# One attention-and-MLP kernel with a new order of its steps: scores of units 3 to 5 in split f16 products, one subtraction moved to VectorE, six sets of fillers fewer

## The chip, the cores and the metric

The kernel runs on one core of a Trainium2 chip. The metric is the device time of one execution in microseconds. TensorE (PE) multiplies matrices, VectorE (DVE) and ScalarE (ACT) work elementwise, GpSimd (POOL) reduces across partitions, and SyncE (SP) issues the DMAs. Each engine takes its instructions strictly in the order in which the program lists them.

## The reference

Attention over 4 batches of 8 heads, 768 positions and 64 dimensions. Each query sees the keys less than 16 positions away and 24 summary keys (maxima of blocks of 32). A two-layer MLP with exact gelu follows.

```python
k_sum = k.reshape(B, H, nb, block, D).max(axis=3)
v_sum = v.reshape(B, H, nb, block, D).mean(axis=3)
scores_l = scale * q @ k.T                    # kept where |i - j| < 16
scores_s = scale * q @ k_sum.T + np.log(block)
scores_all = concat(scores_l_masked, scores_s)
a = np.exp(scores_all - max(scores_all))
a = a / (sum(a) + 1e-9)
attn = a @ concat(v, v_sum)
h = x @ w_in                                  # x: (3072, 512), w_in: (512, 2048)
out = (gelu(h)) @ w_out                       # w_out: (2048, 512)
```

## The kernel before

The attention is cut into 24 units (a batch, four heads, 256 queries); four steps of units 0 to 5 make batch 0. Most products are **split**: an f32 operand becomes a high f16 part and a low one (the rest), and three f16 products (high by high, high by low, low by high) stand for one of f32. The low parts are all made on DVE, and the high ones on ACT: `x_hi` and `x_lo` for the attention's result, `wi_hi`, `wi_lo`, `wo_hi`, `wo_lo` for the weights, `g_hi`, `g_lo` for the gelu's output, and `q_lo`, `k_lo`, `p_lo`, `v_lo` for a unit's queries, keys, probabilities and values. The weights come as 64-bit floats and are turned into f32 by three integer steps each on DVE (`wi_bits`, `wo_bits`, steps 0 to 2); eight chunks of `w_in` and eight of `w_out`.

A unit's scores are either `f_scores` (line 688: 16 matmuls in f32 of a packed copy of the keys that `k_pack` makes on ACT, lines 669 and 675) or `scores` (line 756: 48 matmuls in f16, from `s_q_hi`, `q_lo`, `s_k_hi`, `k_lo`). Before, units 0 to 5 take the first, the others the second. `f_mask` puts the mask into PSUM ahead of them. `evac` copies the scores to SBUF, `maximum` takes the maximum over the partitions on POOL, and it is subtracted either by `m_shift` (line 736: a matmul of -1 with the maximum onto the scores in PSUM, whose result `m_exponent` reads) or by `shift` (line 790: a subtraction in SBUF on DVE, whose result `exponent` reads). Then come `f_sums` or `sums` (denominators), `f_values` or `values` (line 838), and the norm steps `norm_take`, `norm_cross`, `norm_rec`, `norm_spread`, `norm_mult`.

The MLP works on chunks of 256 rows (two units each): `phase1 c i` (lines 915 to 917) makes 256 columns of the hidden layer out of 24 matmuls of 256 columns, and `phase2 c i` (lines 1034 to 1036) makes a quarter of the sum of an output block out of 12 matmuls of 512 columns. `phase2` of quarter n reads the low parts `wo_lo 2n` and `wo_lo 2n+1`. Batches 2 and 3 and the last four chunks' output use a Strassen form (`sp`, line 986, and `so`, line 1199).

`fill` (line 337) is a set of three matmuls of ones into a tile that nobody reads; `setup` issues 16 more of them. They give nothing to the output.

What sets the order is one long text, `ORDER`: a list of some 1,680 steps, written out by hand, each a call of one of the functions named here. It fixes the order on every engine and on the DMA queue of SP. Tiles come from pools with a fixed count of buffers: scores have one tile in PSUM (`pss`) for all units but unit 1, queries one buffer in SBUF, values two.

Of the kernel before, what the change touches and what calls it, by code (L numbers as in the profile page):

```python
# [82 lines left out]
0, wi_bits 2 0, evac 2, load_ind, wi_bits 2 1, fetch_vt 0, sum_vt 0, norm_cross 0, norm_rec 0, maximum 2, fetch_vt 1,
norm_spread 0, m_shift 1, m_exponent 1, fetch_vt 2, load_v 0, sum_vt 1, sum_vt 2, wi_bits 2 2, wi_hi 2, wi_lo 4,
k_pack 3, m_shift 2, fill 12, fetch_w_in 3 3, wi_lo 5, wi_lo 2, wi_bits 3 0, load_v 1, mean_vt, wi_bits 3 1, f_sums 1,
s_load_vs 0, f_values 0, norm_mult 0, m_exponent 2, f_mask 3, load_q 3, f_scores 3, s_load_vs 1, norm_take 1, wi_bits
3 2, x_hi 0, x_lo 0, norm_cross 1, norm_rec 1, f_values 1, fill 13, evac 3, f_sums 2, norm_spread 1, norm_mult 1,
norm_take 2, fetch_w_in 1 1, wi_hi 3, x_hi 1, x_lo 1, fetch_w_out 1 5, norm_cross 2, wi_bits 1 0, norm_rec 2, phase1 0
4, wo_bits 1 0, wi_bits 1 1, load_q 6, maximum 3, m_shift 3, s_q_hi 6, wo_bits 1 1, wi_bits 1 2, phase1 0 2, fetch_k 2
1, prep_k 2 1, load_v 2, m_exponent 3, load_vs 2, wi_hi 1, fetch_w_in 7 3, norm_spread 2, q_lo 6, phase1 0 5, f_values  # L90
2, load_v 3, gelu 0 5, g_hi 0 5, wi_lo 1, load_vs 3, fetch_k 1 3, f_mask 4, wo_bits 1 2, gelu 0 2, load_k 4, g_hi 0 2,
norm_mult 2, k_pack 4, f_sums 3, gelu 0 4, norm_take 3, load_q 4, norm_cross 3, prep_k 1 3, wi_bits 7 0, phase1 0 1,
f_values 3, wi_lo 3, wi_bits 7 1, load_v 4, wo_hi 1, fetch_k 1 2, f_scores 4, x_hi 2, fetch_k 1 1, evac 4, norm_rec 3,
norm_spread 3, g_hi 0 4, prep_k 1 2, gelu 0 1, phase1 0 0, x_lo 2, norm_mult 3, x_hi 3, fetch_w_in 6 2, prep_k 1 1,
f_mask 5, load_vs 4, x_lo 3, g_lo 0 4, g_lo 0 5, fetch_w_out 0 4, fetch_w_out 3 5, wi_bits 6 0, phase1 0 3, maximum 4,
shift 4, wo_lo 1, load_k 5, wi_bits 6 1, g_hi 0 1, g_lo 0 1, gelu 0 0, g_hi 0 0, g_lo 0 0, phase1 1 4, fetch_v 1 2,
load_q 5, gelu 0 3, fetch_k 1 0, phase1 1 5, exponent 4, g_hi 0 3, wi_bits 7 2, f_values 4, gelu 1 5, wo_bits 0 0,
wi_bits 6 2, f_sums 4, g_hi 1 5, g_lo 1 5, wi_hi 7, k_pack 5, wo_bits 0 1, norm_take 4, wi_lo 7, phase1 1 1, load_v 5,
gelu 1 1, g_hi 1 1, g_lo 1 1, wi_hi 6, phase1 1 0, wi_lo 6, prep_v 1 2, load_vs 5, gelu 1 4, f_scores 5, phase1 1 7,
norm_cross 4, gelu 1 0, g_hi 1 0, evac 5, g_hi 1 4, g_lo 0 3, load_k 6, s_k_hi 6, norm_rec 4, wo_bits 0 2, maximum 5,  # L100
norm_spread 4, prep_k 1 0, g_lo 1 0, load_v 6, wo_bits 3 0, fetch_w_out 2 4, phase1 1 6, wo_hi 0, wo_bits 3 1, phase1
1 3, gelu 1 7, phase1 0 7, wo_lo 0, phase2 0 0, shift 5, gelu 1 3, g_hi 1 3, wo_bits 3 2, fetch_w_out 5 5, g_lo 1 3,
norm_mult 4, wo_bits 2 0, exponent 5, f_sums 5, prep_k_end 1 0, f_values 5, gelu 1 6, wo_bits 2 1, load_q 7, norm_take
5, wo_bits 2 2, k_lo 6, g_hi 1 7, g_lo 1 7, wo_hi 3, k_sums 1 0, wo_bits 5 0, wo_lo 3, phase1 0 6, g_lo 0 2, gelu 0 6,
g_hi 0 6, wo_bits 5 1, wo_hi 2, wo_lo 2, fetch_w_out 4 4, f_mask 6, wo_bits 4 0, wo_bits 4 1, norm_cross 5, norm_rec
5, phase1 1 2, gelu 0 7, wo_bits 4 2, wo_hi 4, wo_bits 5 2, wo_hi 5, prep_k_end 1 1, wo_lo 4, wo_lo 5, g_lo 1 4,
scores 6, fetch_v 1 0, phase2 0 1, phase2 0 3, norm_spread 5, load_k 7, s_k_hi 7, phase2 0 2, fetch_v 1 1, phase2 0 5,
g_hi 0 7, fetch_w_out 6 4, x_hi 4, fetch_w_out 7 5, x_lo 4, norm_mult 5, s_q_hi 7, prep_v 1 1, evac 6, maximum 6,
phase2 0 4, load_mask, x_hi 5, x_lo 5, load_v 7, f_mask 7, q_lo 7, gelu 1 2, k_sums 1 1, shift 6, exponent 6, phase1 2
3, g_lo 0 6, wo_bits 6 0, phase1 2 1, load_q 9, k_lo 7, gelu 2 3, wo_bits 7 0, wo_bits 6 1, scores 7, g_hi 1 2, g_lo 1  # L110
2, wo_bits 6 2, wo_bits 7 1, gelu 2 1, s_q_hi 9, wo_hi 6, g_lo 0 7, wo_lo 6, phase1 2 0, load_k 9, wo_bits 7 2, q_lo
9, phase1 2 4, s_k_hi 9, k_lo 9, fetch_v 1 3, gelu 2 0, g_hi 2 0, s_p_hi 6, wo_hi 7, wo_lo 7, phase1 2 6, load_q 11,
load_k 8, phase2 0 6, fetch_k 2 2, prep_v 1 0, g_hi 1 6, g_lo 2 0, s_q_hi 11, prep_v 1 3, q_lo 11, p_lo 6, phase2 0 7,
store 0 0, phase2 1 0, fetch_v 2 1, load_vs 6, load_q 8, evac 7, maximum 7, load_vs 7, s_k_hi 8, gelu 2 6, put 0 0,
g_lo 1 6, prep_v 2 1, sums 6, k_lo 8, fetch_k 2 0, gelu 2 4, g_hi 2 4, v_hi 6, scores 9, norm_take 6, phase2 1 2,
phase2 1 4, prep_k 2 2, shift 7, v_hi 7, v_lo 6, values 6, store 0 1, fetch_k 2 3, g_lo 2 4, g_hi 2 1, prep_k 2 0,
phase1 2 5, s_q_hi 8, q_lo 8, add_mask 9, v_lo 7, scores 8, exponent 7, s_p_hi 7, norm_cross 6, phase2 1 6, p_lo 7,
load_v 8, prep_k 2 3, put 0 1, g_hi 2 6, load_k 11, s_k_hi 11, add_mask 8, load_vs 8, v_hi 8, k_lo 11, norm_rec 6,
norm_spread 6, sums 7, norm_mult 6, x_hi 6, norm_take 7, v_lo 8, phase1 2 2, maximum 9, shift 9, load_q 10, maximum 8,
shift 8, store 1 0, prep_k_end 2 1, values 7, norm_cross 7, norm_rec 7, scores 11, exponent 8, x_lo 6, exponent 9,  # L120
s_q_hi 10, phase2 1 1, load_v 9, norm_spread 7, load_vs 9, gelu 2 5, load_k 10, load_v 11, phase2 1 3, g_lo 2 1,
add_mask 11, load_vs 11, norm_mult 7, g_hi 2 5, g_lo 2 6, s_p_hi 8, p_lo 8, g_hi 2 3, g_lo 2 3, x_hi 7, phase1 2 7,
s_k_hi 10, phase2 1 5, x_lo 7, v_hi 9, maximum 11, phase1 3 0, v_lo 9, gelu 2 7, wt_add 1 0, wt_add 1 1, wt_add 1 2,
wt_hi 1, k_lo 10, sums 8, shift 11, values 8, s_p_hi 9, q_lo 10, norm_take 8, norm_cross 8, load_v 10, gelu 3 0, g_hi
3 0, wt_lo 1, fetch_k 3 1, load_q 12, load_vs 10, norm_rec 8, phase1 3 4, phase2 1 7, wt_add 5 0, p_lo 9, phase1 3 1,
norm_spread 8, norm_mult 8, put 1 0, g_lo 3 0, gelu 2 2, exponent 11, scores 10, wt_add 5 1, fetch_k 3 2, g_hi 2 2,
g_lo 2 2, prep_k 3 1, x_hi 8, store 1 1, wt_add 5 2, g_hi 2 7, g_lo 2 7, gelu 3 4, prep_k 3 2, values 9, wt_hi 5, sums
9, norm_take 9, norm_cross 9, add_mask 10, s_p_hi 11, phase1 3 6, g_lo 2 5, gelu 3 6, load_k 12, phase2 2 1, wt_lo 5,
fetch_v 2 0, s_k_hi 12, norm_rec 9, phase1 3 2, norm_spread 9, put 1 1, gelu 3 1, phase1 3 5, x_lo 8, v_hi 11,
norm_mult 9, prep_k_end 2 0, maximum 10, s_q_hi 12, k_lo 12, shift 10, exponent 10, p_lo 11, q_lo 12, x_hi 9, load_k  # L130
13, s_k_hi 13, v_lo 11, gelu 3 2, k_lo 13, fetch_v 2 2, fetch_v 2 3, g_hi 3 1, phase2 2 3, phase2 2 5, g_hi 3 4,
prep_v 2 0, values 11, k_sums 2 0, k_sums 2 1, sums 11, wt_add 0 0, x_lo 9, phase2 2 7, wt_add 0 1, norm_take 11, sp 2
# [1211 lines left out]
```

## Time and profile before

| what | before |
|---|---|
| median of 3 runs | 575.72 us (575.28 to 575.73) |
| span of the profiled execution | 574.3 us |
| PE busy | 569.0 us (99%) |
| DVE busy | 458.4 us (80%) |
| ACT busy | 379.8 us (66%) |
| POOL busy | 88.7 us (15%) |
| granted TensorE clock, mean | 0.999 |

The span runs from the first to the last instruction of one profiled execution; the median is of timed runs, and lies 1.4 us above that span. A busy time of 99% says that PE almost always had a matmul in it, not that each of them was needed. The shares are means over the whole span: the first 140 us, in which the weights are prepared, are loaded otherwise than the rest.

### The profile page before, as it was taken

What the parts mean: (1) busy time and instruction counts of PE and PEld (TensorE: products, weight loads), DVE (VectorE), ACT (ScalarE), POOL (GpSimd) and SP (SyncE); (2) the same over time, 40 slices, a digit from 0 to 9 for tenths busy, and PEclk for the clock granted to TensorE, in tenths of its full rate; (3) what the DMA queues carried; (4) which work ended last, traced back from release to release, by engine and by line L of the source; (5) the groups of instructions that cost most, each with busy time, mean ns of one, the idle gap of its engine ahead of it and who ended that gap; (6) DMA issues with size and microseconds to landing.
All of it is one profiled execution on the core that took longest, in us unless ns stands there. A gap on an engine that the chain in (4) does not pass through costs nothing.

```text
span 574.3 us, 13533 instructions
## 1 busy us (share of the span) xinstructions
PE 569.0 (99%) x5826; PEld 389.8 (68%) x5826; DVE 458.4 (80%) x617; ACT 379.8 (66%) x642; POOL 88.7 (15%) x42
## 2 busy tenths in 40 slices
...
GB/s 322 395 238 250 342 175 196 274 116 198 159 115 99 141 79 71 115 121 76 103 93 66 72 105 56 60 98 78 23 63 1 21 19 18 1 20 1 2 1 91
DMA packets 28652, 64.27 MB, mean 112 GB/s; under 512 B 2736, under 2 KB 7600, under 8 KB 28592
## 3 DMA queue, kind: packets, MB, share of 16 engines
...
## 4 chain that ended last, share of the span: by engine, by line
PE 95%; DVE 4%; issue 1%; ACT 0%; POOL 0%; DVEq 0%; ACTq 0%; POOLq 0%
PE psy L986 15%; PE pso L1034 12%; PE pso L1035 12%; PE pso L1036 12%; PE psz L986 7%; PE psh L915 4%; PE psh L917 4%; PE psh L916 4%; PE psx L986 4%; PE pso_y L1199 4%; PE psv L838 3%; PE pss L756 3%; PE pss_x L1199 2%; PE pso_fill L337 2%; PE pss L688 1%; PE pso_fill_s L337 1%
## 5 line engine op out<-in xcount | busy, mean ns | idle before, releaser
L785 POOL PARTITION_ALL_REDUCE m<-s x23 | 77.4, 3370 | 303.5 <-DVE s L776 80.9
L1034 PE MATMUL pso<-w_out_h,gg 128*128 128x512 f16 x320 | 121.5, 380 | 0.0
L1035 PE MATMUL pso<-w_out_l,gg 128*128 128x512 f16 x320 | 121.3, 379 | 0.0
L1036 PE MATMUL pso<-w_out_h,gg 128*128 128x512 f16 x320 | 121.3, 379 | 0.0
L986 PEld LDWEIGHTS <-wt 128*128 128x128 f16 x768 | 74.4, 98 | 13.6 <-issue 1.1
L916 PE MATMUL psh<-xos,ww 128*128 128x256 f16 x256 | 69.8, 273 | 0.6 <-DVE xos L895 0.6
L915 PE MATMUL psh<-xos,ww 128*128 128x256 f16 x256 | 69.9, 273 | 0.0
L917 PE MATMUL psh<-xos,ww 128*128 128x256 f16 x256 | 69.8, 273 | 0.0
L986 PE MATMUL psy<-xos,wt 128*128 128x256 f16 x576 | 69.3, 273 | 0.0
L986 PEld LDWEIGHTS <-ww 128*128 128x128 f16 x576 | 55.4, 98 | 11.7 <-issue 0.4
L1036 PEld LDWEIGHTS <-gg 128*128 128x128 f16 x320 | 31.3, 98 | 37.8
L1034 PEld LDWEIGHTS <-gg 128*128 128x128 f16 x320 | 31.3, 98 | 33.2 <-issue 0.8
L1035 PEld LDWEIGHTS <-gg 128*128 128x128 f16 x320 | 31.3, 98 | 31.5
L1018 DVE SCALAR_TENSOR_TENSOR gg<-g,gg 128x512 f16<-128x512 f32 x48 | 34.7, 731 | 11.5 <-ACT gg L1014 11.4
L997 ACT ACTIVATE ww<-psy 128x512 f32<-128x512 f32 x48 | 28.1, 587 | 23.7 <-PE psy L986 23.4
L1041 ACT ACTIVATE ot<-pso 128x512 f32<-128x512 f32 x20 | 11.8, 592 | 29.3 <-PE pso L1036 29.3
L1014 ACT ACTIVATE gg<-g 128x512 f16<-128x512 f32 x48 | 29.4, 625 | 2.7 <-PE pso L1035 2.0
L1004 DVE TENSOR_TENSOR g<-psz,ww 128x512 f32<-128x512 f32 x24 | 16.4, 682 | 18.5 <-PE psz L986 15.8
L1011 ACT ACTIVATE g<-g 128x512 f32<-128x512 f32 x36 | 22.3, 623 | 10.8 <-DVE g L1004 10.7
L915 PEld LDWEIGHTS <-ww 128*128 128x128 f16 x256 | 25.0, 98 | 6.3 <-issue 2.2
L917 PEld LDWEIGHTS <-ww 128*128 128x128 f16 x256 | 25.0, 98 | 3.7 <-issue 0.7
L916 PEld LDWEIGHTS <-ww 128*128 128x128 f16 x256 | 25.0, 98 | 3.4
...
## 6 DMA issues: line engine op xcount, KB each, us to landing
...
```

Of the source, the lines that this page charges most:

```text
L785: nc.gpsimd.partition_all_reduce(out_ap=self.m32, in_ap=self.s32, channels=P, reduce_op=bass_isa.ReduceOp.max)
L915: nc.tensor.matmul(ph[:, e, :], wh, xh, start=(k == 0), stop=False)
L916: nc.tensor.matmul(ph[:, e, :], wh, xl, start=False, stop=False)
L917: nc.tensor.matmul(ph[:, e, :], wl, xh, start=False, stop=(k == NCC - 1))
L986: nc.tensor.matmul(ps[:, e, :], ws, xx, start=(first and e == 0 and k == 0 and m == 0), stop=(k == 1 and m == 2), skip_group_check=True,)
L997: nc.scalar.activation(snaps[b, q, n], split8(acc[b, q, "y"]), AF.Copy)
L1014: nc.scalar.activation(g_part(o // 2, q, 0, slice(o % 2, 4, 2)), g32t[b, q, o], AF.Copy, scale=SC_G)
L1018: nc.vector.scalar_tensor_tensor(out=g_part(o // 2, q, 1, fs), in0=g32t.pop((b, q, o)), scalar=SC_G, in1=g_part(o // 2, q, 0, fs), op0=ALU ...
L1034: nc.tensor.matmul(p, gh, w_out_h[:, f, :], start=(f == 0), stop=False)
L1035: nc.tensor.matmul(p, gh, w_out_l[:, f, :], start=False, stop=False)
L1036: nc.tensor.matmul(p, gl, w_out_h[:, f, :], start=False, stop=(f == NFC - 1))
L1199: nc.tensor.matmul(ps[:, j, :], g, ww_, start=(first and e == 0 and k == 0), stop=(e == 1 and k == 2), skip_group_check=True,)
```

## The change

Only the text `ORDER` changes; no function and no constant does. Against before the list

- leaves out `k_pack 3`, `k_pack 4`, `k_pack 5`, `f_scores 3`, `f_scores 4`, `f_scores 5`, `m_shift 3`, `m_exponent 3`, and the six fillers `fill 1`, `fill 4`, `fill 5`, `fill 6`, `fill 9`, `fill 13`;
- adds `scores`, `s_q_hi`, `q_lo`, `s_k_hi` and `k_lo` for each of units 3, 4 and 5, `shift 3`, `exponent 3`, and the f16 copies of batch 0's summary keys: `prep_k_end 0 0`, `prep_k_end 0 1` (two small DVE instructions each) and `k_sums 0 0`, `k_sums 0 1` (two of ACT each);
- writes all steps in a new order.

Of the diff the head and the tail, cut:

```diff
 ORDER = '''
-fetch_k 0 0, prep_k 0 0, load_m16, f_mask 1, k_pack 0, k_pack 2, load_q 0, fetch_w_in 0 0, wi_bits 0 0, wi_bits 0 1,
-f_mask 0, fill 0, fetch_k 0 1, f_scores 0, fill 1, fill 2, fill 3, fill 4, fill 5, fill 6, fill 7, fill 8, evac 0,
...
+12, h_hi 3 22, so 1 1 0, t_lo 2 4, so 1 0 1, h_gelu 3 0, h_hi 3 11, h_lo 3 22, h_lo 2 12, h_lo 2 11, h_hi 2 3, h_sum 2
...
+1 1, o_sum 3, o_put 3 0, so 4 2 1, so 4 1 0, so 4 0 0, so 4 1 1, o_put 3 1, so 4 2 0, so 4 3 0, o_out 0, o_put 0 0, so
+4 0 1, o_put 2 0, so 4 3 1, o_put 1 0, o_out 1, o_put 2 1
 '''
```

Three places show what moves. (The new file has one line more ahead of the functions, so a function's line is higher by one in it.)

DVE just ahead of the first `phase1`. In before, the last row here is `x_lo 1`, the low part of unit 1's result, and `L424` is `wi_lo`; `L386`, `L391`, `L395` are the three steps that turn a weight into f32.

```order
L424 SCALAR_TENSOR_TENSOR ww<-wt,ww 128x4x256 x3
L386 TENSOR_SCALAR wt<-gg 128x1024
L391 SCALAR_TENSOR_TENSOR wt<-gg,wt 128x1024
L888 TENSOR_TENSOR x32s<-psv_348,dent_290 128x512
L861 STREAM_TRANSPOSE dent_389<-psn_342 128x256
L395 SCALAR_TENSOR_TENSOR wt<-gg,wt 128x1024
L895 TENSOR_TENSOR xos<-x32s,xos 128x512
L877 RECIPROCAL rc_394<-rc_394 128x16
L881 STREAM_TRANSPOSE dent_389<-rc_394 128x512
L888 TENSOR_TENSOR x32s<-psv_401,dent_389 128x512
L861 STREAM_TRANSPOSE dent_431<-psn_424 128x256
L895 TENSOR_TENSOR xos<-x32s,xos 128x512
```

The same place in the new order, on to `shift 3` (`L791`) and the next `wi_lo` (`L425`); `L731` is `q_lo`, `L725` is `k_lo`, and `x_lo 1` is the row with `L896`.

```order
L387 TENSOR_SCALAR wt<-gg 128x1024
L889 TENSOR_TENSOR x32s<-psv_428,dent_354 128x512
L392 SCALAR_TENSOR_TENSOR wt<-gg,wt 128x1024
L896 TENSOR_TENSOR xos<-x32s,xos 128x512
L862 STREAM_TRANSPOSE dent_477<-psn_445 128x256
L731 TENSOR_TENSOR ql_479<-q_4_341,qh_467 128x512
L396 SCALAR_TENSOR_TENSOR wt<-gg,wt 128x1024
L725 TENSOR_TENSOR k_lo_95<-k_4_412,k_hi_93 128x10x64
L878 RECIPROCAL rc_505<-rc_505 128x16
L791 TENSOR_TENSOR s_3_451<-s_3_451,m_3_453 128x1024
L882 STREAM_TRANSPOSE dent_477<-rc_505 128x512
L425 SCALAR_TENSOR_TENSOR ww<-wt,ww 128x4x256
```

`x_lo 1` is row 37 of DVE's list where it was row 30, and `q_lo 4`, `k_lo 4` and `shift 3` stand between it and the next `wi_lo`.

DVE ahead of the first `values` of a unit in split products, that of unit 6. In before, the last row here is `v_lo 6` (row 142 of DVE's list), and `L805` is `p_lo 6`.

```order
L574 TENSOR_SCALAR vm_1608<-vs_920 96x128
L730 TENSOR_TENSOR ql_1610<-q_11_1584,qh_1605 128x512
L805 TENSOR_TENSOR pl_1612<-s_6_1339,ph_1555 128x1024
L933 SCALAR_TENSOR_TENSOR gg<-g_1_6_1123,gg 128x512
L568 TENSOR_REDUCE vs_1658<-vb_1_1641 96x32
L724 TENSOR_TENSOR k_lo_95<-k_8_1586,k_hi_93 128x10x64
L861 STREAM_TRANSPOSE dent_1727<-psn_1660 128x256
L519 TENSOR_REDUCE ks_2_511<-kp_2_1600 128x24
L790 TENSOR_TENSOR s_7_1647<-s_7_1647,m_7_1649 128x1024
L813 SCALAR_TENSOR_TENSOR vl_1676<-v_6_989,vh_1675 128x1024
```

In the new order `v_lo 6` is row 153; this is what stands ahead of it, from the last `wo_lo` (`L485`) on.

```order
L485 SCALAR_TENSOR_TENSOR w_out_l<-wst_1515,w_out_h 128x1024
L569 TENSOR_REDUCE vs_1363<-vb_3_1551 96x32
L575 TENSOR_SCALAR vm_1700<-vs_1363 96x128
L725 TENSOR_TENSOR k_lo_96<-k_9_1619,k_hi_94 128x10x64
L731 TENSOR_TENSOR ql_1725<-q_9_1450,qh_1590 128x512
L934 SCALAR_TENSOR_TENSOR gg<-g_2_4_1557,gg 128x512
L806 TENSOR_TENSOR pl_1761<-s_6_1305,ph_1560 128x1024
L934 SCALAR_TENSOR_TENSOR gg<-g_2_1_1483,gg 128x512
L520 TENSOR_REDUCE ks_2_580<-kp_2_1705 128x24
L569 TENSOR_REDUCE vs_1775<-vb_1_1708 96x32
```

`k_lo 8`, `norm_take 6`, `shift 7` and `q_lo 11` no longer stand ahead of `v_lo 6`; two `g_lo` of chunk 2 do.

PE at the start of unit 6's `values`. In before, they follow a `phase2` (lines 1034 to 1036).

```order
L1035 LDWEIGHTS gg
L1035 MATMUL pso_0_1628<-w_out_l,gg 128x512
L1036 LDWEIGHTS gg
L1036 MATMUL pso_0_1628<-w_out_h,gg 128x512
L838 LDWEIGHTS vh_1675
L838 MATMUL psv_1759<-ph_1555,vh_1675 64x64
```

In the new order they follow the denominators of the same unit, and those follow scores.

```order
L855 MATMUL psn_1829<-pl_1761,ones 32x256
L855 LDWEIGHTS ones
L855 MATMUL psn_1829<-pl_1761,ones 32x256
L839 LDWEIGHTS vh_1767
L839 MATMUL psv_1854<-ph_1560,vh_1767 64x64
```

Scores, denominators and values stand next to each other more often: from the first `phase1` on, PE goes from a large product (`phase1`, `phase2`, `sp`, `so`, masks) to one of these small ones 49 times in before and 23 times in the new order; from the first `values 6` on, 39 and 17 times.

## Rows read from the trace of the kernel before

**Rows 1.** Part 4 of the page: the last chain, by engine.

```profile
PE 95%; DVE 4%; issue 1%; ACT 0%; POOL 0%; DVEq 0%; ACTq 0%; POOLq 0%
```

**Rows 2.** Windows, three stretches: engines' busy us (instructions), clock, DMA share, GB/s.

```profile
5.16:42.57 37.41, 36.44 (x308) 18.91 (x307) 31.97 (x33) 23.00 (x41) 12.43 (x4) 1.00 0.89 334
42.57:139.77 97.20, 97.10 (x1007) 71.86 (x1007) 93.82 (x113) 69.40 (x110) 22.10 (x9) 1.00 0.67 223
139.77:571.00 431.23, 431.23 (x4504) 297.22 (x4502) 332.65 (x473) 285.71 (x491) 52.89 (x16) 1.00 0.22 67
```

**Rows 3.** The chain in order of time: start, us on the chain, what.

```profile
7.50 0.98 PE pss L656 x8
...
17.99 1.05 PE pss L736 x4
...
41.76 0.81 DVE xos L895
...
77.21 1.93 PE pss L688 x32
...
92.89 1.08 PE psv L702 x32
...
234.30 1.31 PE psy L986 x12
235.61 0.81 PE pss L756 x48
236.42 1.42 PE psz L986 x12
```

**Rows 4.** Groups of PE by form: busy us, mean ns of one.

```profile
L337 PE MATMUL pso_fill<-ones 128*64 128x512 f16 x42 | 11.4, 381 | 0.5
...
L337 PE MATMUL pso_fill_s<-ones 128*64 128x512 f16 x16 | 6.6, 599 | 0.9 <-POOL warm L349 0.9
```

**Rows 5.** Groups of DVE by form.

```profile
L790 DVE TENSOR_TENSOR s<-s,m 128x1024 f32<-128x1024 f32 x20 | 24.3, 1217 | 1.9 <-POOL m L785 1.8
...
L933 DVE SCALAR_TENSOR_TENSOR gg<-g,gg 128x512 f16<-128x512 f32 x32 | 23.8, 757 | 2.3 <-ACT gg L927 2.2
...
L724 DVE TENSOR_TENSOR k_lo<-k,k_hi 128x640 f16<-128x640 f32 x18 | 17.1, 948 | 3.2 <-ACT k_hi L664 3.2
...
L730 DVE TENSOR_TENSOR ql<-q,qh 128x512 f16<-128x512 f32 x18 | 13.5, 748 | 0.0
...
L528 DVE TENSOR_TENSOR ks<-ks,ks 128x48 f16<-128x48 f32 x6 | 1.2, 208 | 0.2
```

**Rows 6.** DVE's waits from 5 to 140 us: for whom, us, times, longest.

```profile
DVE wt L386 <- DMA gg<-in_w_in_dram: 2.2, 1, 2.2
DVE rc L877 <- ACT rc L874: 1.4, 1, 1.4
...
DVE w_out_l L484 <- ACT w_out_h L481: 0.8, 1, 0.8
DVE dent L861 <- PE psn L710: 0.8, 2, 0.6
```

**Rows 7.** DVE in order of time, around `v_lo 6`: start, us, instruction, wait ahead.

```profile
136.22 0.45 DVE L861 STREAM_TRANSPOSE dent<-psn 128x256 f32<-128x256 f32 x1 [0.94 <-PE psn L854]
...
138.55 1.22 DVE L813 SCALAR_TENSOR_TENSOR vl<-v,vh 128x1024 f16<-128x1024 f32 x1
139.69 0.68 DVE L933 SCALAR_TENSOR_TENSOR gg<-g,gg 128x512 f16<-128x512 f32 x1
```

**Rows 8.** PE in order of time: a `phase2` at 127.90, `values 6`, and its end.

```profile
127.90 0.38 PE L1034 MATMUL pso<-w_out_h,gg 128*128 128x512 f16 x1
128.11 0.38 PE L1035 MATMUL pso<-w_out_l,gg 128*128 128x512 f16 x1
...
142.19 0.22 PE L838 MATMUL psv<-ph,vh 128*64 128x64 f16 x2
...
568.26 2.78 PE L1199 MATMUL pso_y<-t,gg 128*128 128x256 f16 x24
```

More of the change, by code (lines that the diff above doesn't have):

```diff
@@ L83 @@
[L83 to L132, printed above, removed]
@@ new lines @@
+8, g_lo 2 6, phase2 1 3, s_k_hi 11, phase2 1 5, wt_lo 0, v_hi 9, norm_spread 7, norm_mult 7, x_hi 7, maximum 8, shift
+8, phase1 2 2, exponent 8, k_lo 11, load_k 10, s_p_hi 8, phase2 1 7, gelu 2 2, v_lo 8, x_lo 7, q_lo 11, load_v 11,
+prep_k_end 2 1, v_lo 9, p_lo 8, sums 8, norm_take 8, fetch_k 2 0, scores 11, values 8, gelu 2 5, shift 9, g_hi 2 2,
+g_lo 2 2, exponent 9, load_q 12, put 1 0, add_mask 11, norm_cross 8, load_v 10, g_hi 2 5, s_p_hi 9, maximum 11, phase1
+3 5, s_k_hi 10, norm_rec 8, norm_spread 8, norm_mult 8, phase1 3 3, prep_k 2 0, g_lo 2 5, p_lo 9, k_sums 2 1, s_q_hi
```

263 lines of the change are left out of this document (154 added, 109 removed).

## The prediction, made before the result was known

> **What bounds the kernel now.** I read the chain that ended last first, then busy time by stretch, then the waits inside the stretch that the change rebuilds. The chain lies on PE for 95% of the span and on DVE for 4% [rows 1], and a piece on DVE is the `x_lo 1` at 41.76 [rows 3]. From 42.57 to 139.77 us, that is from the end of `x_lo 1` to the end of `v_lo 6`, PE is busy for 97.10 us of 97.20, and DVE for 93.82 [rows 2]. So there two engines are full at once: PE is the bound, with DVE 3.4 us behind it. Behind 139.77 us PE is busy all the time and DVE for 333 us of 431 [rows 2]; there PE alone counts. The change takes work from PE and gives some to DVE, and it does both ahead of 140 us. The question is at which point DVE becomes the one that is late. All sums are made against the profiled span of 574.3 us; the median of the runs, 575.72, lies 1.4 us above it, and I carry that difference over.
>
> **PE's part.** An `f_scores` takes 1.93 us, a `scores` 0.81 [rows 3]: 1.12 less for each of three units. `m_shift 3` goes with 1.05. Going from a large product into a small one and back costs 0.11: the same 12 matmuls take 1.42 us behind an attention block and 1.31 behind a large product [rows 3]. The new order does so 26 times less from the first `phase1` on (49 to 23), which is 2.6 us at 0.1 each. `f_values 2` (1.08) and `f_mask 4` (half of the 0.98 that two masks took, 0.5) now stand ahead of the first `phase1` [rows 3]. Of the work behind that point, 2.2 (scores of units 4 and 5), 1.05, 1.6 and 2.6 go: 7.5 us. Were PE alone the bound, and did the first `phase1` start when it did, the span would be 566.8.
>
> **The six fillers** are 18 matmuls at 0.381 [rows 4], overlapping, about 0.26 apart: 4.6 us of PE. They stand ahead of the first `phase1`, which waits for `x_lo 1` on DVE in any case (PE was not idle for more than 1 us there only because fillers stood in the gaps). I count them at nothing. What they covered is a wait of PE for DVE and POOL, and that becomes bare.
>
> **DVE's part**, counted up to `v_lo 6`, which `values 6` needs. Ahead of it the new order has, beyond before, three `k_lo` at 0.948, three `q_lo` at 0.748, `shift 3` at 1.217, four small instructions of `prep_k_end` at 0.208 or a little less, and two `g_lo` at 0.757 [rows 5]: 8.6 us. Moved behind it are `q_lo 11`, `k_lo 8`, `shift 7` and `norm_take 6` (0.45 [rows 7]): 3.4 us. Neighbours overlap by 0.08 (138.55 plus 1.22 against a next start at 139.69 [rows 7]), for nine instructions 0.7. So `v_lo 6` comes 4.6 us later on account of work.
>
> On account of waits it comes earlier. DVE was not busy for 5.4 us of the ramp and 3.4 of the stretch behind it [rows 2], of which the named waits of about 0.4 to 2.2 us make 7.6, the four shown 5.2 [rows 6]. The 2.2 for the first chunk of `w_in`: that load now stands third on SP's queue instead of fourth, with unit 0's queries behind it, and `prep_k_end 0 0` fills part; I leave 1.1. The 1.4 for the reciprocal's input: four weight instructions now stand between `norm_take 0` and `norm_rec 0` instead of two, so it goes. Of the 0.8 for PE's denominators I leave 0.3, as PE reaches `f_sums 0` earlier with fewer fillers ahead. The wait for PE ahead of the first `norm_mult` (0.5, one of the smaller ones) goes, since three weight steps and `q_lo 3` stand between. Of the rest, 2.7, I leave half, and I add 0.4 for new ones. That leaves 3.2 and saves 4.4. The bounds: nothing is saved (the same waits in other places), or all but the 1.1 is (6.5).
>
> **Who is queued behind what.** `shift 3` stands in DVE's queue between `k_lo 4` and the `wi_lo` of chunks 3, 1 and 2; it waits for `maximum 3` on POOL, and if that is late, `phase1 0 1` is. `f_sums 3` stands in PE's queue behind two `phase1`, and waits for `exponent 3`. From `scores 3` to `shift 3` there are five or more microseconds of DVE work (`x_lo 0` to `norm_rec 2`), against 1.0 for `evac` and a POOL reduction of 3.2 or more; I count no wait for DVE, and up to 1 us for PE, which lies inside the next sum. `f_mask 3` needs the one score tile, which `m_exponent 2` frees; with `shift` instead of `m_shift`, unit 3 frees it at its `evac`.
>
> **The sum.** `v_lo 6` ended at 138.55 + 1.22 = 139.77, and `values 6` began at 142.19, 2.4 us later [rows 7, 8]. With the new order `v_lo 6` ends at 139.77 + 4.6 - 4.4 = 140.0. PE by itself would be there some 7.5 us sooner than before, at about 134 to 135, so it waits, and `values 6` begins at 140.0: 2.2 us earlier. Behind it PE now has `phase2 1 2` and `phase2 1 4` more (2 x 12 x 0.215 [rows 8] = 5.2), `phase1 2 7` less (24 matmuls of 256 columns, twice the 1.31 of twelve [rows 3], 2.6) and 22 changes into small products less (39 to 17: 2.2): 0.4 more. The end stays as it is: the last product starts at 568.26 [rows 8], and the same steps follow it. Together 574.3 - 2.2 + 0.4 = 572.5, and as a median 573.9, 0.3% faster. So of 7.5 us that PE is spared, 5.7 turn into waits for DVE. A second gate gives less: `phase2 0 6` at 127.90 [rows 8] needs the last `wo_lo`. Ahead of that stand the same `k_lo`, `q_lo`, `shift 3` and `prep_k_end`, two `g_lo` and one `prep_v` (some 1.2) more, and one `g_lo`, `k_lo` and `q_lo` less: 6.7 us later by work, 3.9 earlier by the waits up to there (6.1, of which I leave 2.2). It would start 2.2 us later, since it had 0.6 of room, with 4.9 us less of PE behind it (`phase1 2 7` and 23 changes), so 571.6. The later gate decides.
>
> [...]
>
> **The rivals.**
> PE alone stays the bound, because DVE's waits vanish nearly all and its work fits: the span falls by 4 to 7.5 us, 570.0 as a median in the middle. For it: DVE had 2.4 us of room at `values 6`. Against it: the sum of DVE's work, which no order shortens. 0.08.
> The gain and the waits cancel: of 7.6 us of waits some 2 to 3.5 go instead of 4.4, or one spell at the lower clock falls where PE is the bound; the time is that of before to 1.1 us, 575.7. 0.25.
> Slower: DVE keeps its waits, only elsewhere. Then `v_lo 6` ends at 144.4, `values 6` begins 2.2 us later than before, and 0.4 comes on top: 2.6 us, 578.3. It decides from the point at which less than 2.6 us of waits are saved; for it speaks that DVE now waits for POOL (`shift 3`) and for ACT's `q_hi` and `k_hi` in its fullest stretch. 0.17.
> That the change doesn't do what it says can be left out for the scores, since both forms stand in the trace; for the fillers it is my own count, nothing.
>
> **How the numbers follow.** The forecast (0.3% faster, between 1.1 and 4 us) gets 0.50. About 0.2% is what a measurement of this kernel can tell from no change, 1.15 us. Faster: 0.50 + 0.08 = 0.58; same 0.25; slower 0.17. The range goes from 570.9 (571.8 with all waits but the 1.1 saved, and 0.9 below it towards the first rival) to 577.4 (some two thirds of the way from before to the slower rival), and leaves out about 2 in 10.
>
> **What would show it.** In the profile of the changed kernel: a `scores` of 0.81 for units 3 to 5; PE no longer at 97.1 of 97.2 but with 5 to 6 us of idle time between the first `phase1` and `values 6`, put down to DVE (`wi_lo`, `wo_lo`, `x_lo`, `v_lo`); DVE busy at 97% or more there; `v_lo 6` ending near 140; PE without idle time behind. Wrong would be: PE idle for less than 3 us (the first rival), DVE idle for more than 6 us up to `v_lo 6` (the slower one), a granted clock below 1.00 in the ramp, or waits of PE behind 200 us, where I count none.

## The result, and the profile of the changed kernel

The changed kernel took 579.31 us as a median of 4 runs (578.65 to 581.03), the kernel before 575.73 in the same runs: a ratio of 1.0062 with an interval of 1.0044 to 1.0080, so 0.6% slower. The forecast was 573.9, or 0.3% faster, with a range from 570.9 to 577.4: the kernel got slower instead, and the time lies outside the range.

The profiled execution of the changed kernel took 579.6 us with a span of 577.8, 3.5 us longer than before's span. First the stretches that answer to [rows 2]: the ramp up to the first `phase1` (40.27 us), from there to `values 6` (137.93), on to 175, and to PE's last matmul. The columns are as there: the busy us (instructions) of PE, of PE's weight loads, of DVE, ACT and POOL, then the granted clock, the DMA share and GB/s.

```profile
7.00:40.27 33.27, 31.03 (x330) 16.44 (x329) 31.92 (x36) 21.36 (x40) 15.15 (x5) 0.95 1.04 391
40.27:137.93 97.66, 93.24 (x1021) 70.17 (x1017) 97.15 (x119) 69.87 (x111) 20.70 (x8) 1.00 0.59 198
137.93:175.00 37.07, 33.91 (x417) 21.30 (x414) 28.29 (x40) 26.61 (x45) 9.64 (x3) 0.91 0.48 152
175.00:574.56 399.56, 398.55 (x4082) 278.83 (x4079) 298.34 (x436) 258.18 (x451) 45.06 (x14) 1.00 0.20 61
```

The same stretches of the kernel before, the first three with their ends at its own first `phase1`, its `values 6` and 175:

```profile
7.00:41.11 34.11, 33.66 (x297) 17.40 (x296) 28.96 (x29) 20.93 (x36) 10.97 (x4) 1.00 0.88 335
41.11:142.19 101.08, 100.45 (x1029) 73.50 (x1026) 97.50 (x118) 71.87 (x115) 23.56 (x9) 1.00 0.67 221
142.19:175.00 32.81, 32.81 (x450) 22.83 (x450) 30.49 (x41) 22.86 (x41) 9.65 (x3) 1.00 0.44 146
```

Up to `values 6` things went better than forecast: it began at 137.93 against 142.19 [rows 8], DVE was busy for 97.15 of 97.66 us, and PE idled for 4.4. The loss stands in the third row: PE idles for 3.16 us, and its clock is 0.91 on the mean. The waits of PE that cost most in the whole span (us in total, times, longest):

```profile
PE psn L855 <- DVE pl L806: 3.1, 1, 3.1
PE psn L711 <- ACT s L794: 2.1, 1, 2.1
PE psh L916 <- ACT g L925: 1.5, 4, 0.9
```

The first is `sums 8`: it adds the high part of unit 8's probabilities, and then waits for the low one, `p_lo 8`.

```profile
164.53 0.29 PE L855 MATMUL psn<-ph,ones 128*32 128x256 f16 x4
167.93 0.40 PE L855 MATMUL psn<-pl,ones 128*32 128x256 f16 x4 [3.11 <-DVE pl L806]
```

PE around it, in windows (busy us, granted clock, DMA share, GB/s):

```profile
160.00:164.00 4.00, 4.00 (x29) 1.00 0.03 4
164.00:168.00 4.00, 0.89 (x11) 0.85 0.81 243
168.00:172.00 4.00, 4.00 (x105) 0.50 0.86 333
172.00:174.00 2.00, 2.00 (x13) 0.59 0.04 10
174.00:180.00 6.00, 6.00 (x58) 1.00 0.05 13
```

From 167 us, still inside the wait, to 173 the granted clock is 0.50, in the microsecond behind it 0.67. PE's busy time of each microsecond, times what the clock was short of 1.00 in it, sums to 2.87 us lost here, and to 1.65 in a second spell, at 30 to 34 us of the ramp. (Below, "lost to the clock" is always this sum, and a spell is a stretch with a granted clock below 1.00.)

Why `p_lo 8` was late shows on DVE, whose waits here were 1.1 us at most before:

```profile
152.17 1.22 DVE L569 TENSOR_REDUCE vs<-vb 96x32 f32<-96x1024 f32 x1 [3.72 <-DMA vb<-in_vb_dram]
153.31 0.68 DVE L731 TENSOR_TENSOR ql<-q,qh 128x512 f16<-128x512 f32 x1
153.91 1.21 DVE L777 SCALAR_TENSOR_TENSOR s<-mask_sb,pss 128x1024 f32<-128x1024 f32 x1
...
156.35 1.21 DVE L464 SCALAR_TENSOR_TENSOR wt<-t,wt 128x1024 f16<-128x1024 f32 x1
...
160.97 1.23 DVE L791 TENSOR_TENSOR s<-s,m 128x1024 f32<-128x1024 f32 x1 [2.00 <-POOL m L786]
...
165.53 1.22 DVE L814 SCALAR_TENSOR_TENSOR vl<-v,vh 128x1024 f16<-128x1024 f32 x1
166.66 1.22 DVE L806 TENSOR_TENSOR pl<-s,ph 128x1024 f16<-128x1024 f32 x1
```

`prep_v 2 2` (L569) stands 3.72 us for a block of values. SP's queue, in order of time, shows why: its load (L562) was issued behind transfers into `v` that had to wait for unit 9's values, sent at 141.14.

```profile
141.14 0.43 SPq L604 DMA_DIRECT2D v<-in_vw_dram  x1
145.12 1.65 SPq L632 DMA_DIRECT2D v<-vm  x2
...
147.44 0.38 SPq L562 DMA_DIRECT2D vb<-in_vb_dram  x1
```

`add_mask 8` (L777) stands behind `prep_v 2 2` in DVE's queue, then come POOL's maximum, `shift 8` and the exponent, and `p_lo 8` last, behind two `v_lo`. There is one link more: `maximum 8` began at 157.71 only, 2.6 us behind the end of `add_mask 8` and right behind that of `wt_lo 0` (L464, 156.35 + 1.21; ACT's `q_hi 11`, which POOL's row names, ended 0.1 us before). By the list, the result of a `maximum` takes one of four buffers that it shares with scores, loaded value blocks and the tile that `wt_lo` reads; here three of them were held by the scores of units 8 and 9 and by `maximum 9`.

Summed with the waits that PE's timeline names, from the first `phase1` to PE's last matmul (574.56 against 571.04): the start is 0.84 us earlier, PE's work is 6.3 shorter (534.29 less 8.32 of waits and 2.87 of clock, against 529.93 less 0.57), the waits are 7.75 longer, and the clock loses 2.87. That is +3.5, the difference of the spans.

### The profile page after: what moved, and what is told of

Same layout as the page of the kernel before. It is cut to its first block, busy times and chain, and to the rows that moved or that the text cites. A ratio compares the mean times of both kernels' runs of the same rounds, so it can differ in the third digit from the quotient of the medians.

```text
span 577.8 us, 13613 instructions
## 1 busy us (share of the span) xinstructions
PE 562.8 (97%) x5852; PEld 389.2 (67%) x5852; DVE 457.4 (79%) x628; ACT 378.4 (65%) x646; POOL 91.9 (16%) x42
## 5 line engine op out<-in xcount | busy, mean ns | idle before, releaser
L786 POOL PARTITION_ALL_REDUCE m<-s x23 | 80.6, 3507 | 323.8 <-DVE s L777 111.4
L987 PEld LDWEIGHTS <-ww 128*128 128x128 f16 x576 | 56.0, 98 | 11.3 <-issue 0.5
L917 PEld LDWEIGHTS <-ww 128*128 128x128 f16 x256 | 25.2, 99 | 5.6 <-issue 2.1
L791 DVE TENSOR_TENSOR s<-s,m 128x1024 f32<-128x1024 f32 x21 | 26.9, 1287 | 2.2 <-POOL m L786 2.2
L918 PEld LDWEIGHTS <-ww 128*128 128x128 f16 x256 | 25.2, 99 | 4.3 <-issue 1.2
L814 DVE SCALAR_TENSOR_TENSOR vl<-v,vh 128x1024 f16<-128x1024 f32 x18 | 21.8, 1212 | 8.0 <-ACT vh L811 8.0
```

The lines of the kernel that those rows point to most:

```text
L786: nc.gpsimd.partition_all_reduce(out_ap=self.m32, in_ap=self.s32, channels=P, reduce_op=bass_isa.ReduceOp.max)
L917: nc.tensor.matmul(ph[:, e, :], wh, xl, start=False, stop=False)
L918: nc.tensor.matmul(ph[:, e, :], wl, xh, start=False, stop=(k == NCC - 1))
L987: nc.tensor.matmul(ps[:, e, :], ws, xx, start=(first and e == 0 and k == 0 and m == 0), stop=(k == 1 and m == 2), skip_group_check=True,)
```

## The experiments

Each is compared with the kernel before in the same runs (its medians lay between 575.64 and 576.17). Steps are named as in the list; in the diffs "..." stands for steps that stay.

**Was it the one wait?** Three variants of the changed kernel, and the fillers.

`e1_unblock_p_lo8` moves four things:

```diff
-gelu 2 7, fetch_v 2 2, maximum 9 ... norm_take 7, prep_v 2 2, phase1 2 5 ... x_lo 6 ... wt_lo 0, v_hi 9 ... s_p_hi 8
+gelu 2 7, maximum 9 ... norm_take 7, phase1 2 5 ... wt_lo 0, x_lo 6 ... s_p_hi 8, v_hi 9
-load_v 11, prep_k_end 2 1, v_lo 9, p_lo 8 ... prep_v 2 0 ... prep_v 2 3
+load_v 11, p_lo 8, prep_k_end 2 1, v_lo 9 ... prep_v 2 0, fetch_v 2 2 ... v_lo 11, prep_v 2 2, prep_v 2 3
```

> The changed kernel with four steps moved so that p_lo 8 is ready when TensorE comes to sums 8: the load and the reduction of batch 2's value block 2 (fetch_v 2 2, prep_v 2 2) go behind prep_v 2 0, wt_lo 0 goes ahead of x_lo 6, p_lo 8 ahead of prep_k_end 2 1, v_hi 9 behind s_p_hi 8. Theory A (the loss is one wait: at 164.5 us TensorE waits 3.1 us in sums 8 for p_lo 8, and the granted clock halves behind it for some 5.5 us, which costs another 2.5): p_lo 8 comes 2.5 to 3.5 us earlier, the wait falls under 0.7 us, no clock below 1.00 at 165 to 175 us, and the time falls from 579.3 to 573.0 to 574.5 us. Theory B (the loss sits ahead of the first phase1, in the ramp with fewer fillers and a lower clock): 578.5 to 579.5. Theory C (VectorE is overloaded by the added lows and another of its waits takes this one's place): the wait goes but 577 or more remains.

Measured: 578.34 us (577.41 to 579.91), ratio 1.0050 (1.0033 to 1.0067). The wait in `sums 8` was gone, and no clock below 1.00 at 165 to 175. But behind 140 us other waits had come (us in total, times, longest):

```profile
PE psv L845 <- DVE x32s L895: 2.1, 2, 1.5
PE pss L763 <- DVE s L783: 1.7, 1, 1.7
```

PE waits for a `norm_mult` at 148.96 and for an `add_mask` at 195.46, and its waits behind the first `phase1` sum to 7.6 us instead of 8.3. The clock, too, only moved: it lost 1.67 us at 48 to 52, behind a wait of 2.07 in `f_sums 3`, where the changed kernel's profiled execution had the same wait and lost nothing. Theory A falls, C holds: it was not one wait, it was the next in a row of them. Theory B, a slower ramp, is not what the profile shows: the changed kernel's ramp ended 0.84 us earlier than before's.

`e2_p_lo8_first`:

```diff
-prep_k_end 2 1, v_lo 9, p_lo 8
+p_lo 8, prep_k_end 2 1, v_lo 9
```

> The changed kernel with p_lo 8 alone moved, ahead of prep_k_end 2 1 and v_lo 9 on VectorE (1.6 us of work that stood before it). Theory A: the wait in sums 8 falls from 3.1 to about 1.7 us. If the lower clock follows any wait of this size, the time is 577.9; if it follows only the longer wait, 575.5. Theory B: 579.3 within 0.5.

Measured: 579.69 (579.24 to 581.48). The wait in `sums 8` fell to 1.74 us, as said, and the clock stayed at 1.00 behind it; 0.74 at a `values` at 178 us, 0.85 and 0.67 at 197 us were new. The waits behind the first `phase1` sum to 9.6. So the wait fell as theory A has it and no spell followed, yet the time did not fall: 1.3 us came back as other waits behind the first `phase1`, and where the rest of the 2.9 us of clock went stays open.

`e3_busy_wait`:

```diff
-for n, p in enumerate((self.ph, self.pl)):
+for n, p in enumerate((self.ph,) * (20 if self.u == 8 else 1) + (self.pl,)):
...
-start=(n == 0), stop=(n == 1),
+start=(p is self.ph), stop=(n != (19 if self.u == 8 else 0)),
```

> The changed kernel with the wait kept and TensorE kept busy in it: sums 8 repeats its first pass (ph against ones) 19 more times, 3.2 us of matmuls at 0.17 us a pass whose result is overwritten by the last one. Theory A: p_lo 8 comes as late as before, so the 3.1 us stay, but the clock stays at 1.00 behind it and the time falls by the cold clock's price alone, 2.3 to 2.9 us, to about 576.7. If the clock falls for another reason than TensorE's idling: 579.3.

Measured: 581.24 (580.08 to 581.83), 1.9 more instead of 2.6 less. The mechanism came out, the clock was 1.00 from 164 to 180 us. But the profiled execution came to its first `phase1` at 44.18 instead of 40.27, with 6.8 us lost to the clock at 10 to 15 and 21 to 32 us, ahead of anything that the edit touches. From there to the end it was 1.7 us shorter than the changed kernel. Why that ramp was worse stays open; only one of the four executions left a trace, so whether the others had the same ramp is not shown. This run proves little.

`e4_fillers_back`:

```diff
-fill 7, fill 12 ... m_shift 0 ... f_values 1
+fill 7, fill 1, fill 4, fill 5, fill 6, fill 12 ... m_shift 0, fill 9 ... f_values 1, fill 13
```

> The changed kernel with the six removed sets of fillers (0.76 us each, 4.6 us of TensorE, they compute nothing) put back: four behind fill 7, one behind m_shift 0, one behind f_values 1. Theory A: the ramp ends on VectorE's x_lo 1, so nothing changes, 579.3 within 0.5 us; up to 1.5 more if two of them stand on the path. Theory B: the clock of the ramp rises above 0.95 and the time falls to 576 to 578.

Measured: 583.19 (582.08 to 584.19), 3.9 more. Both theories missed it: `m_shift 0` came at 19.37 instead of 16.11, and the first `phase1` at 45.72. Where I put them the fillers stood on the path.

**What does each part cost alone?** Five kernels in the old order.

`e5_f16_old_order` (unit 3 shown; 4 and 5 alike):

```diff
-k_pack 3 ... wi_lo 2 ... load_v 1, mean_vt, wi_bits 3 1 ... load_q 3, f_scores 3
+s_k_hi 3 ... wi_lo 2, k_lo 3 ... load_q 3, load_v 1, mean_vt, s_q_hi 3, wi_bits 3 1, q_lo 3 ... scores 3
+prep_k_end 0 0, prep_k_end 0 1, k_sums 0 1, k_sums 0 0
```

> The kernel before with the first part alone: scores of units 3 to 5 in split f16 products, in the old order. Each k_pack becomes s_k_hi plus k_lo, each s_q_hi and q_lo stand a few steps ahead of their scores, prep_k_end and k_sums of batch 0 are added. TensorE is spared 3 x 1.12 us plus the changes into small products, VectorE gets 3 x 0.95 + 3 x 0.75 + 0.8 = 5.9 us ahead of v_lo 6. Theory D (formed from the four runs above: VectorE and the chains through it are the gate up to about 200 us, so what TensorE is spared becomes waits, and waits bring the lower clock): 575 to 577.5, with TensorE's waits behind the first phase1 up from 0.6 to 3 us or more. Theory E (the new order is what costs, the parts themselves gain): 572 to 573.5.

Measured: 579.93 (578.53 to 580.97), ratio 1.0061 (1.0040 to 1.0081). This part alone costs 3.8 us, as much as the whole change and more than either theory had. PE's waits from 41 us on:

```profile
PE pss L764 <- DVE k_lo L732: 1.7, 1, 1.7
PE psh L923 <- ACT xos L900: 1.3, 1, 1.3
PE pss L764 <- DVE ql L738: 1.1, 2, 0.8
PE psh L924 <- DVE xos L903: 0.5, 1, 0.5
```

Three of them are `scores` that wait for their own lows. Behind the 1.7 and behind the 1.3 the clock fell, and 1.57 and 1.71 us were lost.

`e6_shift3_old_order`:

```diff
-m_shift 3 ... m_exponent 3
+shift 3 ... exponent 3
```

> The kernel before with the second part alone: m_shift 3 and m_exponent 3 on TensorE and ScalarE become shift 3 on VectorE and exponent 3. TensorE -1.06 us, VectorE +1.14 and a wait for maximum 3 on POOL, which shift 3 meets directly in this order. Theory D: VectorE stands 2 to 3 us for the maximum, behind it wi_bits, wi_lo and with them phase1: 577 to 579. Theory E: 575 to 576.

Measured: 576.55, ratio 1.0006 (0.9997 to 1.0015): no difference. PE's waits behind the first `phase1` went up by 2.4 us and its work there down by 1.2, the first `phase1` came 1.4 us earlier, and the clock stayed at 1.00.

`e7_six_fillers_out`:

```diff
-fill 1, fill 4, fill 5, fill 6 ... fill 9 ... fill 13
```

> The kernel before with the third part alone: the six sets of fillers taken out (4.6 us of TensorE work that computes nothing). By the prediction's count they are hidden: 575.7 within 0.5. By what it cost to put them back into the new order (+3.9): the ramp hangs on TensorE, and the time falls to 572 to 573.5, unless the granted clock of the ramp falls below 1.00 for the waits that become bare, which gives back up to 3.5 us of it.

Measured: 576.24 (ratio 1.0011, 0.9984 to 1.0038). No difference in the median, as counted: in the profiled execution 3.4 us were lost to the clock at 16 to 24 us, all ahead of the first `phase1`, which came at 40.32, 0.8 us earlier than before's. But the ten runs go from 574.47 to 583.24: two took 582.7 and 583.2, at a mean clock of 0.98, where the others had 0.993 to 0.997. Of the kernel before, with its fillers, no run on record took more than 577.8. What those two runs lost, and where, left no trace.

`e8_all_parts_old_order` is the three diffs together.

> The kernel before with all three parts (scores in f16, shift 3, six sets of fillers out) in the old order: what is left to the changed kernel is the order alone. Theory D: 576 to 580, so that the order is worth nothing or little either way. Theory E: 570 to 573, and the order alone costs 6 us or more.

Measured: 583.69 (581.08 to 585.91), 7.5 more than before, above either expectation. The changed kernel has the same parts and stands at 3.6 more, so by the medians its new order gives back 3.9. In the profiled execution (585.91, the slowest) the extra comes from the ramp, where the clock lost 10.1 us from 16 to 38:

```profile
7.00:16.00 9.00, 7.75 (x61) 4.20 (x59) 6.47 (x10) 3.89 (x7) 3.22 (x1) 1.00 1.04 396
16.00:38.00 22.00, 21.75 (x98) 10.73 (x95) 16.11 (x17) 10.34 (x20) 6.92 (x2) 0.53 0.94 358
```

`e12_f16_shift_old_order` is e5 and e6 together, with all fillers.

> The run e8_all_parts_old_order (583.69) with the six sets of fillers kept, that is f16 scores and shift 3 in the old order. Alone, taking the fillers out cost nothing (576.24 against 576.17). If they matter in company of the f16 scores (in e8 the clock was at its lower level from 16 to 38 us and cost 10 us of TensorE work, and the first phase1 began at 45.9 instead of 40.7): 579 to 581. If they are worth nothing here either: 583.7 within 0.8, and f16 and shift together cost 7.5.

Measured: 580.08 (577.44 to 580.57), 4.0 more than before. So the fillers, worth nothing in the median alone, were worth 3.6 us in company of the f16 scores: the fastest run of e8 (581.08) is slower than the slowest of e12.

**Is it VectorE's load?** GpSimd was to take the lows of units 4 and 5.

`e9_lows_on_pool` (on the changed kernel):

```diff
+POOL_LO = (4, 5)
...
-nc.vector.tensor_tensor(out=self.ql, in0=self.q32, in1=self.qh, op=ALU.subtract)
+eng = nc.gpsimd if self.u in POOL_LO else nc.vector
+eng.tensor_tensor(out=self.ql, in0=self.q32, in1=self.qh, op=ALU.subtract)
```

and `k_lo` alike.

> [...] Theory D (VectorE is full from 41 to 148 us, and TensorE's waits there and the lower clock behind them follow from that): the waits of TensorE behind the first phase1 fall from 8.3 us by 2 to 3, the time to 575.5 to 577.5. Theory F (the waits are chains of latencies: loads, GpSimd's maxima, ScalarE; VectorE's load doesn't matter): 579.3 within 0.8, or more, where a maximum comes later.

Measured: 595.01; `e10_pool_and_unblock`, the same with the moves of e1, 594.89.

> The run before this one together with the four moves of e1_unblock_p_lo8 (578.34). Theory D: VectorE is spared 3.1 us up to 110 us and its own waits of 148 to 161 us are gone, so TensorE's waits fall to 3 to 5 us and the time to 573.5 to 576, at or below the kernel before. Theory F: 578.3 within 0.8.

`e11_f16_pool_old_order`, the same on e5, took 587.34.

> The run e5_f16_old_order (f16 scores of units 3 to 5 in the old order, 579.93) with k_lo and q_lo of units 4 and 5 on GpSimd. Its TensorE waited there for just these: 0.75 and 0.39 us for q_lo, 1.67 for k_lo, and lost 1.6 us to a lower clock behind the last. Theory D: 576 to 577.5. Theory F, or GpSimd is slower than 2.5 us for one: 579 to 582.

All three missed, for a reason of their own. GpSimd's rows of e9:

```profile
42.36 1.65 POOL L633 COPY v<-w_out_h 24x1024 f32<-24x1024 f32 x1 [1.07 <-DMA v<-in_vw_dram]
53.43 1.14 POOL L740 TENSOR_TENSOR ql<-q,qh 128x512 f16<-128x512 f32 x1 [9.43 <-issue]
54.55 1.38 POOL L733 TENSOR_TENSOR k_lo<-k,k_hi 128x640 f16<-128x640 f32 x1
```

The subtractions take 1.1 to 1.4 us, but GpSimd stood 9.43 ahead of the first, and PE 7.59 for it. So these three runs say nothing on the load.

So the lows were left out, or made dead weight.

`e13_no_lows_old_order` (on e5) and `e14_no_lows_new_order` (on the changed kernel); the low by high and high by low products of the scores of units 3 to 5 are computed with the high halves:

```diff
 def k_lo(self):
+    if self.u in NO_LO:   # (3, 4, 5)
+        self.kl = self.kh
+        return
```

and `q_lo` alike.

> The run e5_f16_old_order (579.93) without k_lo and q_lo of units 3 to 5: their scores read the high halves in place of the low ones, so TensorE does the same 48 matmuls and VectorE is spared 5.1 us; the low parts of these scores are left out of the computation. If the lows are what costs (as load or as latency): 572 to 574, no wait of TensorE at scores 4 and 5. If the cost lies in the rest of the f16 form (ScalarE's high copies, prep_k_end, the earlier load_q 3): 577 to 580.

Measured: 573.46 (573.15 to 574.28), ratio 0.9964 (0.9951 to 0.9978), a clock of 1.00, no wait at `scores`. So PE's saving is worth 2.2 us where nothing else is asked for it, and the lows cost 6.0 in this order (3.8 + 2.2).

> The changed kernel without k_lo and q_lo of units 3 to 5 (left out of the computation as in e13_no_lows_old_order). Theory D (VectorE's load): VectorE is full from 41 to 148 us in the changed kernel, so with 5.1 us less of it TensorE's waits behind the first phase1 fall from 8.3 to 3 to 5 us, and the time from 579.3 to 573 to 576. Theory F (the latency of the lows to TensorE): no wait of TensorE names a low of units 3 to 5 here, so 578.5 to 580.

Measured: 576.52 (574.97 to 578.94), ratio 1.0019 (1.0001 to 1.0037): 2.8 less than the changed kernel, a little above D's range. The ten runs lie in two groups, six from 575.0 to 577.1 and four from 578.4 to 578.9; the profiled one (575.1) is of the first. In it the wait in `f_sums 3` is gone and the waits behind the first `phase1` sum to 6.4 us. That in `sums 8` is still there, with 2.7 us, and no lower clock followed it. So the lows make most of what the new order loses, too.

`e15_dead_lows_f32` (on before): subtractions of the same sizes, read by nobody.

```diff
+wi_lo 2, dead_k 3 ... wi_bits 3 1, dead_q 3 ... norm_take 3, dead_k 4 ... wi_bits 7 0, dead_q 4
+norm_take 4, dead_q 5 ... wi_lo 7, dead_k 5; prep_k_end 0 0, prep_k_end 0 1
```

> The kernel before with the lows as dead weight: VectorE does subtractions of the size of k_lo and q_lo at the places where e5_f16_old_order has them, and prep_k_end of batch 0, 5.9 us in all; nothing reads them, and the scores stay in f32. Theory D: VectorE had 3.4 us of room up to 140 us and 2.4 at values 6, so some 1 to 4 us of waits come to TensorE, 577 to 580. Theory F: nobody waits for the results, 575.7 to 576.5.

Measured: 576.95 (576.21 to 577.75), ratio 1.0021 (1.0012 to 1.0031), between the two theories. Of the 6.0 us, DVE's load makes 1.3 by itself.

`e17_new_order_f32`:

```diff
-s_k_hi 3, k_lo 3, s_q_hi 3, q_lo 3, scores 3
+norm_take 1, k_pack 3 ... f_scores 3
```

(units 4 and 5 alike, behind `exponent 3` and `wo_hi 1`).

> The changed kernel with the first part undone: scores of units 3 to 5 in f32 again (k_pack instead of high and low copies, a few steps ahead of each f_scores; prep_k_end and k_sums of batch 0 out), shift 3, the missing fillers and the new order kept. TensorE gets 3.4 us back, VectorE loses 5.9. If the new order is worth in itself what it gave back in company of the other parts (4.4 us): 570.5 to 573, faster than both. If it only repairs what the f16 scores break: 575 to 577.

Measured: 586.49. Neither. My places for `k_pack` made ACT late (it stood 4.2 us ahead of `k_pack 5`, and PE 4.3 us for the gelu behind it, at 84 us), and 9.4 us were lost to the clock. What the new order is worth without the f16 scores stays open.

**Does idling bring the lower clock?** `e18_fillers_in_waits` (on e5):

```diff
-f_values 3 ... scores 4 ... scores 5
+f_values 3, fill 20 ... scores 4 ... fill 21, fill 22, scores 5
```

> The run e5_f16_old_order (579.93) with fillers (0.76 us each, they compute nothing) where its TensorE waited for lows: one ahead of scores 4 (waits of 0.75 us), two ahead of scores 5 (0.39 and 1.67). The waits stay as long as the lows come late, but TensorE idles for under 0.9 us at a time. If its idling brings the lower clock: no spell at 81 to 86 us, which cost 1.57, and 578.0 to 578.8; the spell at 44 to 48 behind x_hi 1 stays. If the clock falls for another reason: 579.9 within 0.7.

Measured: 578.35 (577.31 to 579.72), ratio 1.0042 (1.0028 to 1.0057), 2.5 over before where e5 is 3.8. The two intervals overlap, so the 1.3 us between them are not clear of the noise; but 2.3 us of PE work that computes nothing did not make the kernel slower. What tells is the clock. First e5, then e18, in the same windows of PE:

```profile
80.00:82.00 2.00, 0.33 (x14) 0.90 0.00 0
82.00:86.00 4.00, 4.00 (x60) 0.62 0.62 213
```

```profile
80.00:82.00 2.00, 1.04 (x19) 1.00 0.00 0
82.00:86.00 4.00, 4.00 (x76) 1.00 0.62 213
```

With the fillers 76 matmuls instead of 60 fit into the same 4 us. The spell at 43 to 47, where no filler stood, remained in this execution. Of the six runs of e18 four had a mean clock of 1.00, of e5's four none had more than 0.997: so the spells come in some executions of a kernel and not in others.

**Can order avoid it?** `e16_f16_two_units_early_lows` (on before; unit 3 stays in f32):

```diff
-load_k 4 ... k_pack 4 ... gelu 0 4 ... norm_take 3, load_q 4 ... f_scores 4
+load_k 4, load_q 4 ... s_k_hi 4 ... gelu 0 4, s_q_hi 4 ... norm_take 3, k_lo 4, q_lo 4 ... scores 4
-g_hi 1 5, g_lo 1 5, wi_hi 7, k_pack 5, wo_bits 0 1 ... f_scores 5
+g_hi 1 5, s_q_hi 5, s_k_hi 5, g_lo 1 5, q_lo 5, k_lo 5, wi_hi 7, wo_bits 0 1 ... scores 5
```

(and `prep_k_end` and `k_sums` of batch 0).

> The kernel before with f16 scores for units 4 and 5 alone, in the old order but with the lows earlier: q_lo 4 straight behind k_lo 4, s_q_hi 5 and s_k_hi 5 ahead of wi_hi 7 and q_lo 5, k_lo 5 ahead of wo_bits 0 1; unit 3 stays in f32, prep_k_end of batch 0 stands behind norm_take 0, all fillers stay. TensorE is spared 2 x 1.12 plus some 0.2, VectorE gets 4.0 us (by e15_dead_lows_f32 its load is worth some 0.9 of 1.3). If the price of the f16 scores was the waits for late lows and the clock behind them: no wait at scores 4 and 5, a clock of 1.00, and 573.8 to 575.2, at or below the kernel before. If VectorE's load is what costs where TensorE is spared: 576.5 to 578.

Measured: 576.98 (576.12 to 577.95), ratio 1.0022 (1.0013 to 1.0031). The clock was 1.00 and no `scores` waited, yet the kernel was 1.1 us slower than before, as the second expectation has it. What DVE made earlier for the scores it made later for the weights and the results:

```profile
PE psh L925 <- DVE ww L432: 1.3, 1, 1.3
PE psh L924 <- DVE xos L903: 1.1, 2, 0.6
```

From the first `phase1` to `values 6` DVE was busy for 100.2 us of 102.7, where before it had 97.5 of 101.1.

## Why the prediction was wrong, point by point

**What bounds the kernel.** Right as a reading of [rows 2], and too short. I took DVE for a bound up to `values 6`, and PE alone behind it. In the changed kernel PE reaches `values 6` 4.3 us earlier, and then DVE, or a chain through DVE, is late again at 165, in e1 at 149 and 195. That DVE was busy for 333 us of 431 behind 140 us [rows 2] hid this. I read it so: chains of load, DVE, POOL, DVE, ACT, DVE were covered before by PE's lateness, not by DVE's speed.

**PE's part.** Forecast 7.5 us less behind the first `phase1`, measured 6.3. Mis-sized by 1.2. The scores of units 4 and 5, counted as 2.2, gave 1.8 to 1.9 less work behind the first `phase1` in e13 and e5, and `m_shift 3` gave its share in e6 (1.2). So the rest, some 0.8, lies in the changes into small products (2.6, from a price of 0.11 read off one pair of rows) or in what moved ahead of the first `phase1` (1.6); which of them stays open.

**The fillers at nothing.** Right in the median for the kernel before (e7), though two of its ten runs were some 7 us longer. Wrong as a general count: with the f16 scores in the old order their absence cost 3.6 us (e8 against e12).

**DVE's part and `values 6`.** Forecast 140.0, measured 137.93; "5 to 6 us of idle time" of PE up to there, measured 4.4; "DVE busy at 97% or more", measured 99.5%. This step held, even on the good side.

**Who is queued behind what.** I allowed up to 1 us for `f_sums 3` behind `exponent 3`; it waited 2.08. I named nobody behind the moved `fetch_v 2 2` and `prep_v 2 2`, and that was the 3.72 us of DVE, with `add_mask 8` behind it. It is the omission that the list of moved steps would have shown: `prep_v 2 2` now stood four DVE steps behind its load.

**The step that failed** is "the end stays as it is", with "PE without idle time behind". From `values 6` to PE's end I added 0.4 us to before's 428.85; it took 436.63. Of these 7.8 us, 0.4 is the counted work, 4.2 are idle time of PE, 2.9 the clock, and 0.3 I can't place. Of the idle time 3.2 us and of the clock all 2.9 lie ahead of 175 us, at `p_lo 8`; the end behind 200 us did stay nearly as it was, with waits of 0.8. The gain at `values 6` (4.3) was lost behind it, and more than that.

**The clock.** In the trace of before the granted clock is 1.00 in every microsecond up to PE's last matmul at 571.04. So the spell in the rival of 0.25 was my estimate and shown by no row, and so were the 3.5 us that e7's expectation allows for one: they are 16 x (599 - 381) ns from [rows 4], and these 16 matmuls ran at a granted clock of 1.00 (0.94 to 7.50 us). The runs showed other sizes. In the changed kernel's ramp the clock was 0.95 and 1.65 us were lost. In the ramp of e7 3.4 us were lost and the time stayed; in that of e8 it was 10.1, and the first `phase1` came 4.8 us later than before's. What I missed is that the waits into which I let PE's saving turn, 5.7 us by my own sum, lie where PE is the bound, and that a spell can follow a wait there. With fillers in the waits e18 had a clock of 1.00 at 82 to 86 us, where e5 had 0.62. Yet one cannot count on either outcome: of the 20 waits of over 1.2 us behind the first `phase1` in the profiled executions (e9 to e11 and e17 left out), 7 were followed by a spell. Six of these cost 1.57 to 1.71 us, the one in the changed kernel 2.87. The 3.17 us in e4 were followed by none.

**The rivals.** The nearest in time was the slower one (578.3), but its mechanism did not happen: it had `v_lo 6` at 144.4. The nearest in kind was the rival that I gave 0.25, a spell at the lower clock where PE is the bound. It came, with 0.50 at 167 to 173 us, and beside it 4.2 us of waits that no case of mine had behind `values 6`.

**Where the parts' gain went.** In the old order, the f16 scores are worth 2.2 us without their lows (e13), and the lows take 6.0. PE from the first `phase1` to its last matmul, in the profiled executions of e5 and e13 (busy us, granted clock, DMA share, GB/s):

```profile
40.70:575.94 535.24, 530.71 (x5552) 0.99 0.30 95
```

```profile
38.75:569.25 530.50, 527.52 (x5552) 1.00 0.30 96
```

With the lows the start is 1.95 us later, PE idles 1.55 longer and loses 3.27 to the clock, and its work is the same to 0.1: 6.7 in all, the difference of the two spans. This execution of e5 is its slowest and has two spells; the other three, by their mean clock of 0.997, lost some 1.7 (an estimate, 0.003 of the span). As DVE's load alone, with nobody waiting for them, the lows took 1.3 (e15). Put early enough, they delay the weights instead (e16). PE is spared 1.12 us a unit, DVE gets 0.95 + 0.75 at [rows 5]'s durations, in a stretch where it has 3.6 us of 101 to give. None of the 16 variants that compute everything beat the kernel before. That the lows are what costs is shown for the old order, and in the new one for most of the loss (e14); what the new order is worth by itself is not.
